# Attention loop of a two-layer MQA + SwiGLU kernel: exponentials in fixed tiles, and waits declared away

## The chip, the cores and the metric

One core of a Trainium2 chip runs the kernel. The metric is device time in microseconds of one execution of the program; less is better. TensorE is called PE (its weight loads PEld), VectorE DVE, ScalarE ACT, GpSimd POOL and SyncE SP, as in the profile. Each engine takes its own instructions in order and is held only by semaphores that other instructions raise.

## The reference

The input is x, 2048 rows of 448 floats. Two layers, with the same weights, each run attention and then a feed-forward:

```python
def _A_ref(x, wq, wk, wv, wo):          # H = 16 heads of Dh = 28; one k and one v for all heads
    q = (x @ wq).reshape(B, S, H, Dh).transpose(0, 2, 1, 3)
    k = x @ wk
    v = x @ wv
    scores = einsum("bhqd,bkd->bhqk", q, k) * (Dh ** -0.5)
    p = softmax(scores)
    o = einsum("bhqk,bkd->bhqd", p, v)
    return o.transpose(0, 2, 1, 3).reshape(B, S, H * Dh) @ wo
def _B_ref(x, w_gate, w_up, w_down):
    return (silu(x @ w_gate) * (x @ w_up)) @ w_down
for _ in range(2):
    x = x + _A_ref(layernorm(x), wq, wk, wv, wo)
    x = x + _B_ref(layernorm(x), w_gate, w_up, w_down)
```

So each layer takes 16 x 2048 x 2048 exponentials, 67 million.

## The kernel before

**Stages.** `forward` runs, for each of the two layers, projections of q, k and v (`Attention.project`), the attention loop (`Attention.scores`) and the feed-forward (`FeedForward.rest`). It is traced twice: the first version is the one that runs; a second one, with exact row maxima, stands in a branch that is taken only if the first finds a sum out of range.

**The attention loop.** Queries are taken in 16 groups `GR`: a group is a block of 512 query rows and four heads. Keys are taken in 16 tiles of 128. A *cycle* is two key tiles of one group, so a group has 8 cycles (`NT // 2`) and a layer 128. Scores are computed transposed: keys on the partitions, queries along the row. For one key tile, four heads run side by side in four row groups of PE (32 rows each, DH = 28 and the rest for the split parts); each of the four products is the sum of three matmuls, because q and k are split in a high and a low part. That makes 12 matmuls of 32 x 128 by 512 (line 590, in `tile_scores`).

**Where scores go.** PSUM has eight banks. Two tiles `threes[0]` and `threes[1]` hold three banks each: heads 0 to 2 of the first and of the second key tile of a cycle. Head 3 goes to a single bank; two single banks (6 and 7) change places from cycle to cycle (`singles`).

**The exponentials,** in `cycle(m)`, per cycle and in this order on ACT: line 607 takes the first key tile's single bank to `pt1`, line 608 its three banks to `pt` (1536 elements on each of 128 partitions), line 611 the second key tile's three banks, and line 612 the second single, in place in SBUF, after DVE has copied it there out of its bank (line 610). The copy frees the bank early. Results lie in SBUF tiles `pt` (128 x 1536) and `pt1` (128 x 512) from a pool `at{layer}` with four buffers each. A key tile takes one buffer of each, so a buffer is used again after two cycles.

**P-V.** After the scores and exponentials of cycle m have been issued, `pv(m - 1, singles(m)[0])` is issued: 8 matmuls (line 639) that multiply the exponentials of the previous cycle with `vsb`, the four heads side by side in column groups, into the single bank that line 607 of cycle m has just read. Then DVE takes the result out: at the first cycle of a group by a copy into a fresh accumulator (line 646), at the seven others by an addition (line 648). `vsb` has a column of ones, so the sum of exponentials comes along. After a group's last cycle `post` normalizes the accumulator (POOL line 677, DMA).

**What PE runs, in order:** the 12 scores of the first key tile, the 12 of the second, the 8 matmuls of the previous cycle's P-V, and so on. After certain cycles an out-projection of a finished block of rows (line 575, `outproj`) stands between two cycles; there are three in a layer's loop, and the fourth follows it.

**Who waits for whom in the loop.**
- Line 607 waits for the last scores of the first key tile; line 611 for those of the second; line 612 for the copy at line 610, which waits for the second key tile's single.
- The first scores wait until line 608 of the cycle before has read `threes[0]`, the second until line 611 has read `threes[1]`.
- P-V waits for the exponentials of the cycle before and, since it overwrites the bank, for line 607 of its own cycle.
- The second key tile's single scores of the next cycle overwrite the bank that P-V used, so they wait for the sum at line 648 or 646.

**How waits come about.** The order on each engine is that of the program text (`manual_schedule`). The framework follows which instruction reads and writes which tile and gives each instruction the waits that these need. It also does so between instructions of one engine, and does not drop a wait because another wait implies it. An instruction carries one wait; further ones stand in an event instruction (EVENT_SEMAPHORE) ahead of it. Before the change the exponentials also wait for the exponential that wrote the same buffer two cycles earlier, and the sum for the sum before it and for line 607, which read the same bank.

Of the kernel before, what the change touches and what calls it, by code (L numbers as in the profile page):

```python
# [8 lines left out]
F32 = mybir.dt.float32  # L9
F32R = mybir.dt.float32r  # L10
AF = mybir.ActivationFunctionType
ALU = mybir.AluOpType
# [3 lines left out]
P = 128  # L16
# [11 lines left out]
SCALE = DH ** -0.5  # L28
# [27 lines left out]
def forward(  # L56
# [14 lines left out]
    nc = tc.nc  # L71
# [16 lines left out]
    phase, banks, threes, live, turn = ExitStack(), [], [], set(), {}  # L88
# [33 lines left out]
    def halves(name):  # L122

        return pers.tile([P, 2, 512], F32R, tag="halves", name=name, bufs=2)
# [204 lines left out]
    class Attention:  # L329
# [224 lines left out]
        def scores(self, ff):  # L554
            next(switch)
            with tc.tile_pool(name=f"at{self.layer}", bufs=1, reuse_waits="tile") as wp:
                woh = wp.tile([P, NG, D], F32R, name="woh")
                wol = wp.tile([P, NG, D], F32R, name="wol")
                on, accs, pts = {}, {}, {}
# [23 lines left out]
                def tile_scores(n, three, one):  # L583

                    i, kt = divmod(n, NT)
                    q, k, ks = qts[i % 3], keys[kt // 4], slice(P * (kt % 4), P * (kt % 4) + P)
                    for z, (kp, part) in enumerate(((0, 0), (1, 0), (0, 1))):
                        for j in range(4):
                            js = slice(32 * j, 32 * j + 32)
                            nc.tensor.matmul(  # L590
                                three[:, j, :] if j < 3 else one, k[js, kp, ks], q[js, part, :],
                                start=(z == 0), stop=(z == 2), tile_position=(32 * j, 0),
                            )
                    pt = wp.tile([P, 3, 512], F32, name="pt", bufs=4)
                    pt1 = wp.tile([P, 512], F32, name="pt1", bufs=4)
                    pts[n] = [*(pt[:, j, :] for j in range(3)), pt1]
                    return pt, pt1

                def singles(m):

                    return banks[6 + m % 2], banks[7 - m % 2]

                def cycle(m):

                    a, b = singles(m)
                    pt, pt1 = tile_scores(2 * m, threes[0], a)
                    nc.scalar.activation(pt1, a, AF.Exp, scale=SCALE)
                    nc.scalar.activation(pt, threes[0], AF.Exp, scale=SCALE)  # L608
                    pt, pt1 = tile_scores(2 * m + 1, threes[1], b)
                    nc.vector.tensor_copy(pt1, b)  # L610
                    nc.scalar.activation(pt, threes[1], AF.Exp, scale=SCALE)  # L611
                    nc.scalar.activation(pt1, pt1, AF.Exp, scale=SCALE)

                def between_cycles(m):

# [17 lines left out]
                def pv(m, to):  # L633

                    i, u = divmod(m, NT // 2)
                    for y in range(2):
                        n = 2 * m + y
                        for j in range(4):
                            nc.tensor.matmul(  # L639
                                to[32 * j : 32 * j + 32, :], vsb[:, n % NT, :], pts[n][j],  # L640
                                start=(y == 0), stop=(y == 1), skip_group_check=True,
                            )
                        del pts[n]
                    if u == 0:
                        accs[i] = halves("o2").bitcast(F32)
                        nc.vector.tensor_copy(accs[i][:, 0, :], to)
                    else:
                        nc.vector.tensor_tensor(accs[i][:, 0, :], to, accs[i][:, 0, :], ALU.add)  # L648
                    if u == NT // 2 - 1:
                        due[m + 3] = post(i)  # L650

                def post(i):

                    c, g = GR[i]
                    out2 = accs.pop(i)
                    oraw, rb = out2[:, 0, :], out2[:, 1, :]
                    rs = wp.tile([P, 16], F32, name="rs", bufs=2)
                    for j in range(4):
                        nc.sync.dma_start(rs[32 * j : 32 * j + 32, :], oraw[32 * j + DH : 32 * j + DH + 1, :])

                    def rest():
                        if fine is not None:
                            under = wp.tile([P, 16], F32, name="under", bufs=2)
                            for bound, op in ((LIMIT, ALU.is_lt), (1.0 / LIMIT, ALU.is_gt)):
                                nc.vector.tensor_scalar(under, rs, bound, None, op)
                                nc.vector.tensor_tensor(fine, fine, under, ALU.mult)
                        nc.vector.reciprocal(rs, rs)
                        rd = dram.tile([4, 512], F32, name="rd", bufs=2)
                        nc.sync.dma_start(rd.rearrange("j (p n) -> (j p) n", n=16), rs)
                        nc.sync.dma_start(rb, rd[:, None, :].to_broadcast([4, 32, 512]))  # L670
                        if g == 0:
                            on[c] = (
                                wp.tile([P, NG, 512], F32R, name="onh"),
                                wp.tile([P, NG, 512], F32R, name="onl"),
                            )
                        oh, ol = on[c]
                        nc.gpsimd.tensor_tensor(rb, oraw, rb, ALU.mult)  # L677
                        split(oh[:, g, :], ol[:, g, :], rb)
                        if g == NG - 1 and c < NC - 1:
                            todo.append(c)  # L680

                    return rest
# [37 lines left out]
                for m in range(last):  # L720
                    i, u = divmod(m, NT // 2)
                    if u == 2 and 2 < i + 2 < len(GR):
                        self.stack(i + 2)
                    if u == 3 and 2 < i + 2 < len(GR):
                        self.parts(i + 2)
                    if u == 4 and 2 < i + 2 < len(GR) and not full:
                        self.rows(i + 2)
                    if i in (2, 3) and u == 4:
                        load_wo(i - 2)
                    if m == NT // 2 and ff.nxt:  # L730
                        ff.nxt.below(nc.sync)
                    if u == 4 and 10 < i <= 11 + FG:
                        ff.W[i - 11] = weights(i - 11)
                    cycle(m)
                    if m:
                        pv(m - 1, singles(m)[0])
                    elif not full:
                        self.maxima(NC - 1, banks[6])
                    if m in due:
                        due.pop(m)()  # L740
                    if m in aside:
                        aside[m]()
                    between_cycles(m)
                pv(last - 1, banks[6])
                self.lent = None
                next(switch)
# [258 lines left out]
    for c in range(1, NC):  # L1005
        fs, got = norm_steps(c)
        n = 4 * c - 4
# [38 lines left out]
```

## Time and profile before

| | |
|---|---|
| median of three runs | 1998.7 us |
| the three runs | 1998.66, 1998.7, 2002.25 us |
| profiled execution | 2002.23 us, of which its span 2000.5 us |
| mean granted TensorE clock | 0.997 |
| instructions recorded | 44597 |
| attention loops (first score to last P-V) | about 64 to 571 us and 1055 to 1561 us |

An *execution* is the device's own time; the *span* is from the first to the last recorded instruction of the profiled one. A record of ACT or DVE in an ordered view has a start, a duration, the engine, the source line, the operation, the tile written and the tiles read, and in brackets the idle time of the engine before it with what ended it. Start plus duration is the end. Records of one engine may overlap, as an engine begins an instruction before the one ahead has written its last result. `x8` behind a line counts merged instructions. Lines with `ACTq` or `DVEq` are instructions of an engine's queue that do no arithmetic; the page does not count them as busy.

### The profile page before, as it was taken

How to read it: one execution, taken by the hardware profiler on the slowest of the kernel's cores; microseconds unless marked ns; L12 is line 12 of the kernel's file. 1: busy time of each engine (PE TensorE's matmuls, PEld its weight loads, DVE VectorE, ACT ScalarE, POOL GpSimd, SP SyncE). 2: the span in 40 equal slices, each digit the busy share in tenths (PEclk: the TensorE clock that was granted, in tenths of full speed). 3: DMA queues.
4: the chain of work that ended last, by engine and by line, in shares of the span. 5: the costliest groups of instructions: out<-in, count | busy, mean ns of one | idle time of the engine just before them, and what ended most of it. 6: DMA issues, size and time to landing. Idle time of an engine off the chain costs nothing.

```text
span 2000.5 us, 44597 instructions
## 1 busy us (share of the span) xinstructions
PE 1978.4 (99%) x18517; PEld 1337.5 (67%) x18517; DVE 785.4 (39%) x1370; ACT 1277.5 (64%) x2142; POOL 560.4 (28%) x611
## 2 busy tenths in 40 slices
PE   9999999999999999999999999999999999999998
PEld 7544545445468999999884444454454789988887
DVE  6444443443543222322464334535444332222322
ACT  4899797997953333333349998979979433333332
POOL 5222213122214233333351221122221233233320
PEclk9999999999999999999999999999999999999999
DMA  5101020021211011110031010200212100011102
GB/s 164 52 24 37 12 57 17 22 51 32 44 42 35 25 32 31 32 31 22 12 100 35 25 31 12 62 13 26 52 37 58 45 16 22 26 31 32 32 1 76
DMA packets 126343, 75.30 MB, mean 38 GB/s; under 512 B 69656, under 2 KB 109976, under 8 KB 126136
## 3 DMA queue, kind: packets, MB, share of 16 engines
q1 hardware_dynamic: 124584, 71.20, 12.9%
q8 instruction: 146, 2.39, 0.5%
q10 hardware_dynamic: 1552, 1.20, 0.2%
q14 instruction: 61, 0.50, 0.1%
HBM read 54.01 MB, written 17.83 MB: 36 GB/s over the span
## 4 chain that ended last, share of the span: by engine, by line
PE 94%; DVE 2%; POOL 1%; ACT 1%; DMA 1%; issue 0%; ACTq 0%; POOLq 0%; SPq 0%; DVEq 0%
PE bank L318 39%; PE bank L639 24%; PE three L590 17%; PE bank L590 6%; PE bank L298 4%; PE three L575 2%; PE bank L575 2%; PE bank L248 1%; POOL xl L279 0%; DMA qd<-stage 0%; ACT pt L611 0%; DVE xn L230 0%; DMA xn<-xt 0%; DMA xres<-in_A_x_dram 0%; DVE xres L579 0%
## 5 line engine op out<-in xcount | busy, mean ns | idle before, releaser
L639 PE MATMUL bank<-pt,vsb 128*32 128x512 f32 x4096 | 493.2, 598 | 0.5
L590 PE MATMUL bank<-qstack,keys 32*128 32x512 f32 x1536 | 483.8, 424 | 1.7 <-DVE xres L579 1.7
L590 PE MATMUL three<-qstack,keys 32*128 32x512 f32 x4608 | 448.8, 420 | 1.4 <-ACT stage L524 1.0
L318 PE MATMUL bank<-xh,wgh 64*128 64x512 f32 x1728 | 443.7, 391 | 4.0 <-ACT xh L278 1.4
L590 PEld LDWEIGHTS three<-qstack,keys 32*128 32x128 f32 x4608 | 258.1, 182 | 282.2 <-ACT pt L608 185.2
L611 ACT ACTIVATE pt<-three 128x1536 f32<-128x1536 f32 x256 | 383.1, 1496 | 0.0
L608 ACT ACTIVATE pt<-three 128x1536 f32<-128x1536 f32 x256 | 379.4, 1482 | 0.0
L318 PE MATMUL bank<-xh,wgl 64*128 64x512 f32 x1404 | 366.2, 391 | 0.0
L318 PE MATMUL bank<-wdh,h 64*128 64x448 f32 x1792 | 333.1, 365 | 1.2 <-ACT h L904 0.8
L318 PE MATMUL bank<-xl,wgh 64*128 64x512 f32 x1296 | 331.4, 391 | 2.6 <-POOL xl L279 2.1
L903 DVE TENSOR_TENSOR sg<-bank,sg 128x512 f32<-128x512 f32 x112 | 77.5, 692 | 511.8 <-ACT sg L902 502.6
L318 PEld LDWEIGHTS bank<-xh,wgh 64*128 64x128 f32 x1728 | 261.2, 185 | 22.5 <-POOL xh L288 2.2
L639 PEld LDWEIGHTS bank<-pt,vsb 128*32 128x32 f32 x4096 | 107.1, 109 | 249.1 <-issue 152.6
L810 POOL TENSOR_TENSOR xres<-stage,xres 128x448 f32<-128x448 f32 x108 | 127.9, 1204 | 506.0 <-ACT stage L809 506.0
L648 DVE TENSOR_TENSOR o<-bank,o 128x512 f32<-128x512 f32 x224 | 155.0, 692 | 280.5 <-PE bank L639 276.4
L610 DVE COPY pt<-bank 128x512 f32<-128x512 f32 x256 | 176.9, 691 | 205.5 <-PE bank L590 203.1
L318 PEld LDWEIGHTS bank<-wdh,h 64*128 64x128 f32 x1792 | 244.3, 185 | 14.7 <-issue 2.3
L590 PEld LDWEIGHTS bank<-qstack,keys 32*128 32x128 f32 x1536 | 243.9, 183 | 7.8 <-DVE xres L579 3.6
L677 POOL TENSOR_TENSOR o<-o 128x512 f32<-128x512 f32 x32 | 41.2, 1289 | 739.7 <-DMA o<-rd 431.6
L325 ACT COPY seen<-bank 128x1 f32<-128x1 f32 x664 | 81.4, 163 | 255.0 <-PE bank L318 249.8
L318 PEld LDWEIGHTS bank<-xh,wgl 64*128 64x128 f32 x1404 | 214.7, 185 | 13.1
L318 PE MATMUL bank<-wdl,h 64*128 64x448 f32 x896 | 218.2, 368 | 0.0
(130 smaller groups left out, 2323.5 us busy)
## 6 DMA issues: line engine op xcount, KB each, us to landing
o<-rd SPq DMA_DIRECT2D x32, 256.0 KB
qd<-stage SPq DMA_DIRECT2D x32, 224.0 KB
qraw<-qd SPq DMA_DIRECT2D x128, 56.0 KB
wdr<-in_B_w_down_dram SPq DMA_DIRECT2D x28, 224.0 KB
xt<-tb SPq DMA_DIRECT2D x96, 56.0 KB
wr<-in_B_w_gate_dram SPq DMA_DIRECT2D x28, 192.0 KB
wr<-in_B_w_up_dram SPq DMA_DIRECT2D x28, 192.0 KB
xn<-xt SPq DMA_DIRECT2D x6, 768.0 KB
```

Source lines behind the costliest of these rows:

```text
L298: nc.tensor.matmul(po, a, b, start=(i == 0), stop=(i == len(seq) - 1))
L318: nc.tensor.matmul(po, a, b, start=start, stop=stop, skip_group_check=True)
L325: nc.scalar.copy(seen[:, i : i + 1], po[:, 0:1])
L575: nc.tensor.matmul(po[:, 0:D], a[:, g, ts_], b[:, g, :], start=(g + z == 0), stop=(g == NG - 1 and z == 2))
L590: nc.tensor.matmul(three[:, j, :] if j < 3 else one, k[js, kp, ks], q[js, part, :], start=(z == 0), stop=(z == 2), tile_position=(32 * j, 0),)
L608: nc.scalar.activation(pt, threes[0], AF.Exp, scale=SCALE)
L610: nc.vector.tensor_copy(pt1, b)
L611: nc.scalar.activation(pt, threes[1], AF.Exp, scale=SCALE)
L639: nc.tensor.matmul(to[32 * j : 32 * j + 32, :], vsb[:, n % NT, :], pts[n][j], start=(y == 0), stop=(y == 1), skip_group_check=True,)
L648: nc.vector.tensor_tensor(accs[i][:, 0, :], to, accs[i][:, 0, :], ALU.add)
L810: nc.gpsimd.tensor_tensor(r, s, r, ALU.add)
L903: nc.vector.tensor_tensor(sg, pg[1], sg, ALU.mult)
```

## The change

Three things are changed, all in `Attention.scores`.

1. The exponentials' tiles are allocated once, before the loop, as four pairs `pt0` to `pt3` and `single0` to `single3`; key tile n of the loop uses pair n % 4. Before, each key tile asked the pool for the next of four rotating buffers.
2. Dependencies are declared away: of each exponential on the one two cycles earlier in the same buffer; of the copy at line 610 on line 612 two cycles earlier; of each sum (line 648) on the sum of the cycle before; and of each sum or first copy (648, 646) on line 607 of the cycle in which it runs.
3. Lists keep the instructions that these declarations name.

```diff
-                    pt = wp.tile([P, 3, 512], F32, name="pt", bufs=4)
-                    pt1 = wp.tile([P, 512], F32, name="pt1", bufs=4)
+                    pt, pt1 = bufs[n % 4]
                     pts[n] = [*(pt[:, j, :] for j in range(3)), pt1]
                     return pt, pt1
 
+                exps, sums = {}, {}
+                bufs = [
+                    (wp.tile([P, 3, 512], F32, name=f"pt{y}"), wp.tile([P, 512], F32, name=f"single{y}"))
+                    for y in range(4)
+                ]
+
...
                     a, b = singles(m)
                     pt, pt1 = tile_scores(2 * m, threes[0], a)
-                    nc.scalar.activation(pt1, a, AF.Exp, scale=SCALE)
-                    nc.scalar.activation(pt, threes[0], AF.Exp, scale=SCALE)
+                    es = [nc.scalar.activation(pt1, a, AF.Exp, scale=SCALE)]
+                    es.append(nc.scalar.activation(pt, threes[0], AF.Exp, scale=SCALE))
                     pt, pt1 = tile_scores(2 * m + 1, threes[1], b)
-                    nc.vector.tensor_copy(pt1, b)
-                    nc.scalar.activation(pt, threes[1], AF.Exp, scale=SCALE)
-                    nc.scalar.activation(pt1, pt1, AF.Exp, scale=SCALE)
+                    copy = nc.vector.tensor_copy(pt1, b)
+                    es.append(nc.scalar.activation(pt, threes[1], AF.Exp, scale=SCALE))
+                    es.append(nc.scalar.activation(pt1, pt1, AF.Exp, scale=SCALE))
+                    exps[m] = [e.ins for e in es]
+                    for new, old in zip(exps[m], exps.get(m - 2, ())):
+                        tc.declare_no_dep(new, old, reason="P-V, which read the buffer, waited for the old one")
+                    if m > 1:
+                        tc.declare_no_dep(copy.ins, exps[m - 2][3], reason="P-V, which read it, waited for that")
...
                     if u == 0:
                         accs[i] = halves("o2").bitcast(F32)
-                        nc.vector.tensor_copy(accs[i][:, 0, :], to)
+                        f = nc.vector.tensor_copy(accs[i][:, 0, :], to)
                     else:
-                        nc.vector.tensor_tensor(accs[i][:, 0, :], to, accs[i][:, 0, :], ALU.add)
+                        f = nc.vector.tensor_tensor(accs[i][:, 0, :], to, accs[i][:, 0, :], ALU.add)
+                        if m + 1 in exps:
+                            tc.declare_no_dep(f.ins, sums[m - 1], reason="scores, ahead of this P-V, waited for the sum")
+                    sums[m] = f.ins
+                    if m + 1 in exps:
+                        tc.declare_no_dep(f.ins, exps[m + 1][0], reason="P-V waited for the bank's exponential")
```

## The prediction

> **What bounds the kernel now.** I read the page first, for the share of each engine and for the slices, then the stretches of the attention loop, then its instructions in order of time.
>
> ```profile
> span 2000.5 us, 44597 instructions
> ...
> PE 1978.4 (99%) x18517; PEld 1337.5 (67%) x18517; DVE 785.4 (39%) x1370; ACT 1277.5 (64%) x2142; POOL 560.4 (28%) x611
> ...
> ACT  4899797997953333333349998979979433333332
> ```
>
> The change touches only the two attention stages, where ACT stands at 7 to 9 tenths (it drops where out-projections stand between cycles); over the whole span it has 64%, a mean over two kinds of stage. PE's 99% says little: its matmul ends are modelled and the records overlap. The next view is busy time in the eight stretches of uninterrupted attention cycles, four per layer, cut at the first exponential of a cycle (first stretch and sum; columns are length, then busy us and count of PE, PEld, DVE, ACT, POOL).
>
> ```profile
> 65.02:201.41 136.39, 136.01 (x1475) 58.97 (x1479) 55.66 (x98) 136.39 (x149) 26.23 (x25) 1.00 0.10 29
> ...
> sum 914.93, PE 913.74 PEld 395.01 DVE 411.87 ACT 914.60 POOL 182.42; mean PE 114.22 PEld 49.38 DVE 51.48 ACT 114.33 POOL 22.80
> ```
>
> ACT is busy 914.60 of 914.93 us. A layer has 128 cycles; three hold an out-projection and the last has no successor, so the stretches hold 2 x 124 = 248 cycles: 914.93 / 248 = 3.689 us each. Is that ACT's own rate, or another engine's pace with ACT's records stretched over it? The cycles just after an out-projection tell, where PE is well ahead (ACT in order of time: start, duration):
>
> ```profile
> 477.17 0.61 ACT L607 ACTIVATE pt<-bank 128x512 f32<-128x512 f32 x1
> 477.64 1.47 ACT L608 ACTIVATE pt<-three 128x1536 f32<-128x1536 f32 x1
> 478.97 1.49 ACT L611 ACTIVATE pt<-three 128x1536 f32<-128x1536 f32 x1
> 480.30 0.67 ACT L612 ACTIVATE pt<-pt 128x512 f32<-128x512 f32 x1
> 480.82 0.64 ACT L607 ACTIVATE pt<-bank 128x512 f32<-128x512 f32 x1
> ...
> 484.48 0.67 ACT L607 ACTIVATE pt<-bank 128x512 f32<-128x512 f32 x1
> ...
> 488.14 0.69 ACT L607 ACTIVATE pt<-bank 128x512 f32<-128x512 f32 x1
> ```
>
> By starts, L607 comes every (488.14 - 477.17) / 3 = 3.657 us. But its record grows, 0.61, 0.64, 0.67, 0.69. By ends (477.78, 481.46, 485.15, 488.83) the distance is 11.05 / 3 = **3.683 us**. Starts run ahead of what gets finished, so the ends are the rate. At finer digits the same ends repeat at 3.685 in most cycles; I use 3.685. So 248 cycles at ACT's own rate take 913.9 us, and they took 914.93: all other waits together cost about **1.05 us** of the loop.
>
> The other engines stand close behind, which the chain of waits on the page, 94% PE, hides. One cycle (all engines, in order of time):
>
> ```profile
> 301.52 1.92 PE L639 MATMUL bank<-pt,vsb 128*32 128x512 f32 x16
> ...
> 303.38 0.50 PE L590 MATMUL three<-qstack,keys 32*128 32x512 f32 x3
> ...
> 303.57 0.69 DVE L648 TENSOR_TENSOR o<-bank,o 128x512 f32<-128x512 f32 x1 [1.25 <-PE bank L639]
> ...
> 303.96 0.39 PE L590 MATMUL bank<-qstack,keys 32*128 32x512 f32 x1
> 304.12 0.19 PEld L590 LDWEIGHTS three<-qstack,keys 32*128 32x128 f32 x3 [0.21 <-ACT pt L611]
> ...
> 304.31 0.18 PEld L590 LDWEIGHTS bank<-qstack,keys 32*128 32x128 f32 x1
> ...
> 304.47 0.60 ACT L607 ACTIVATE pt<-bank 128x512 f32<-128x512 f32 x1
> ...
> 304.88 0.39 PE L590 MATMUL bank<-qstack,keys 32*128 32x512 f32 x1
> 304.96 1.45 ACT L608 ACTIVATE pt<-three 128x1536 f32<-128x1536 f32 x1
> 305.20 0.16 PEld L639 LDWEIGHTS bank<-pt,vsb 128*32 128x32 f32 x8 [0.36 <-ACT pt L607]
> ...
> 305.31 0.69 DVE L610 COPY pt<-bank 128x512 f32<-128x512 f32 x1 [1.05 <-PE bank L590]
> ```
>
> **Loop A, through the sum:** P-V starts at 301.52 and ends at 303.44; the sum L648 starts 0.13 later, ends at 304.26, and 0.05 later (304.31) the single's weights for the second scores load, since those scores overwrite the bank that the sum reads; the last score starts at 304.88 and the next P-V at 305.20. That is 3.68 us, as long as ACT's rate. **Loop B, through L607:** P-V 301.52, scores 303.38, the first twelve end at 304.35, L607 starts 0.12 later, takes 0.60 to 0.69, and P-V may follow 0.05 after its end: 1.86 + 0.97 + 0.12 + 0.60 + 0.05 = 3.60, with the long record 3.69. So three loops are within 0.1 us of each other, and ACT's is the one that cannot shrink.
>
> **The change part by part.** What can go is seen in the instructions of each line (event instructions that carry a wait of their own, counts, ns min/median/max, first and last start):
>
> ```profile
> L607 ACTq EVENT_SEMAPHORE  x254: 17/17/1029, 64.2 to 1556.6; - x127
> ...
> L611 ACTq EVENT_SEMAPHORE  x252: 17/17/17, 73.1 to 1557.3; - x126
> ...
> L612 ACTq EVENT_SEMAPHORE  x252: 17/17/17, 73.9 to 1558.2; - x126
> ...
> L648 DVEq EVENT_SEMAPHORE  x224: 21/1881/2069, 73.2 to 1560.2; - x112
> ...
> L646 DVEq EVENT_SEMAPHORE  x32: 21/50/50, 71.4 to 1537.2; - x32
> ```
>
> An instruction with more than one wait is preceded by such an event. With the wait for the exponential two cycles back gone, each of L607, L611, L612 has one wait left (PE, PE, the copy): about 758 ACT events go. L648 keeps PE alone: 224 go. L646, the first sum of eight, loses one wait but its tile must still come free.
>
> *Price of an event on the path.* L648 behind its event starts 0.13 after the last P-V; L610, which has none, starts at 305.31, 0.04 after the matmul that ends at 305.27. So 0.09 us per sum. For ACT the row without an event is the cast below: matmul end 64.03, start 64.06, 0.03 against L607's 0.12, again 0.09 (0.06 to 0.09, rounding included).
>
> ```profile
> 63.64 0.39 PE L298 MATMUL bank<-xh,wl 128*128 128x512 f32 x1
> ...
> 64.06 0.59 ACT L523 CAST q<-bank 112x512 fp32r<-112x512 f32 x1 [2.32 <-PE bank L298]
> ```
>
> Summed blindly, 224 x 0.09 = 20 us on DVE and 254 x 0.09 = 23 us on ACT. But loop A falls to 3.59 and loop B to 3.51-3.60, and ACT's 3.685 then covers both. What is left to win there is the 1.05 us.
>
> *Does ACT's rate itself fall?* The 758 events are 17 ns each, 13 us if they took engine time. They do not: the first two cycles of each layer have none for L611 and L612 (first one at 73.1), and yet:
>
> ```profile
> 65.02 0.61 ACT L607 ACTIVATE pt<-bank 128x512 f32<-128x512 f32 x1
> ...
> 68.69 0.63 ACT L607 ACTIVATE pt<-bank 128x512 f32<-128x512 f32 x1
> ...
> 72.35 0.66 ACT L607 ACTIVATE pt<-bank 128x512 f32<-128x512 f32 x1
> ```
>
> Ends 65.63, 69.32, 73.01: 3.69 per cycle, the same rate without them. I take 0 here; the bounds are 0 and, by starts, 8.0 us (rival 1).
>
> The Trainium skill (Perfetto Trace Analysis, section "DVE / Act Engine Instruction") says why in a rule that speaks against this change: a semaphore wait is served in a queue ahead of the engine, and the record runs from the first element to the acknowledged write. By that rule a wait long satisfied costs a saturated engine nothing; the stretched records with even ends agree.
>
> *The rest.* The copies' dropped wait: L610 already has a single wait's delay, and L612, which needs it, starts 1.6 us after it ends (302.32 to 303.93): 0. Restarts after the six out-projections and the two layer starts: there L607 waits on PE in the open, 8 x 0.06 = 0.5 us at most, 0.3 taken. First sums of eight (L646): if their event stays, 0.13 against the others' 0.04, 32 x 0.09 = 2.9 us without cover, 0 under ACT's slack of 0.09 per cycle. Fixed tiles: same bytes, same four buffers; ACT's ends are equally spaced whichever buffer is written: 0. Feed-forward and projections: untouched.
>
> **Sum:** about 0.7 of the 1.05 us (one or two long cycles will remain) plus 0.3 = **-1.0 us**. The profiled execution is 2002.23 us, span 2000.5 and 1.7 around it: span 1999.5, execution 2001.2. It lies 3.5 above the median of the runs, 1998.7, so for a median **1997.7 us**, -0.05%. Its own range is 1996.5 to 1999.
>
> **Rivals.**
> 1. *Starts are the rate.* If ACT can hold the 3.657 us of starts once no event stands between exponentials, 914.93 - 248 x 3.657 = 8.0 us go: 1998.7 - 8.0 - 0.3 = **1990.4**. For it: loops A and B would allow it (3.59, 3.60). Against: the growing records, and the first cycles without events.
> 2. *Nothing is taken away*, because another dependency still makes the instruction take two waits: events stay, **1998.7**. It cannot be excluded from the trace; it differs little from the forecast.
> 3. *The stage boundary, slower.* The tiles now live from before the loop to its end, in another layout, and the feed-forward's tiles lie over them. If a tile on its path comes to lie over a buffer read by the last P-V where an earlier one was read a cycle before, it waits one cycle longer, 3.7 us in each layer: 1998.7 + 7.4 = **2006.1**. It decides once the added delay exceeds 2 us per layer. Against it: what the feed-forward's first copies wait for is the out-projection, which PE runs after the last P-V.
>
> ```profile
> ACT xh L278 <- PE bank L575: 8.5, 2, 4.5
> ```
>
> **How the numbers follow.** Forecast 0.58, rival 1 0.25, rival 2 0.05, rival 3 0.12. About 0.2%, 4 us, is what a measurement of this kernel can tell from no change. Faster: rival 1, 0.25. Same: forecast and rival 2, 0.63. Slower: rival 3, 0.12. The range takes in the forecast, rivals 1 and 2: 1990.3 to 2001, the upper end with 2 us for a boundary that costs a little.
>
> **What would show it.** Right: events of L611, L612 and L648 gone; the sum 0.04 after P-V; L607's record near its longest (0.70) in most cycles, since ACT alone now paces; L607's ends still 3.685 apart; 248 cycles in 914 us. Wrong: ends under 3.67 (rival 1); event counts unchanged (rival 2); a later first feed-forward matmul relative to the last P-V (rival 3); or P-V waiting for something other than L607.

## The result and the profile after

The changed kernel takes 1999.16 us (median of 12 runs, 1997.58 to 2001.18); the kernel before, run beside it, 2000.99 us (12 runs, 1998.66 to 2003.03). The ratio is 0.9992, with a 95% interval from 0.9983 to 1.0: no change that can be told with confidence, with a lean of 0.1% towards faster. The profiled execution of after took 1999.73 us, its span 1998.0; that of before 2002.23 and 2000.5. Some 2.5 us have to be found in the traces.

In after the lines have moved: the four exponentials are 612 (was 607), 613, 616 and 617 (was 612), the copy is 615, the sum 658 (was 648), the first sum of a group 656, P-V 649 (was 639). Scores stay at 590.

**What was taken away.** The lines of after, with their instructions (count, ns min/median/max, first and last start):

```profile
L612 ACT ACTIVATE single<-bank x256: 597/754/762, 65.3 to 1554.7; 128x512 f32<-128x512 f32 x128
L612 ACTq EVENT_SEMAPHORE  x8: 17/17/17, 64.5 to 1461.5; - x8
...
L616 ACT ACTIVATE pt<-three x256: 1461/1614/1633, 67.2 to 1556.5; 128x1536 f32<-128x1536 f32 x128
...
L617 ACT ACTIVATE single<-single x256: 642/799/808, 68.5 to 1557.8; 128x512 f32<-128x512 f32 x128
...
L658 DVEq EVENT_SEMAPHORE  x2: 21/21/21, 568.6 to 1558.2; - x2
...
L656 DVEq EVENT_SEMAPHORE  x28: 21/21/21, 130.7 to 1535.4; - x28
```

The first single's exponential had 254 events and has 8; lines 616 and 617 had 252 each and have no row for events at all; the sum had 224 and has 2. So 750 events went from ACT and 222 from DVE, and the declarations do what they say. The first exponential's own record was shorter in before:

```profile
L607 ACT ACTIVATE pt<-bank x256: 597/627/700, 65.0 to 1556.6; 128x512 f32<-128x512 f32 x128
```

**The rate of the loop.** Two rows of the first exponential, from the ordered view of ACT, 37 uninterrupted cycles apart, in after:

```profile
65.34 0.61 ACT L612 ACTIVATE single<-bank 128x512 f32<-128x512 f32 x1
...
201.56 0.76 ACT L612 ACTIVATE single<-bank 128x512 f32<-128x512 f32 x1
```

and in before, where the first of the two rows is the one at 65.02 in the prediction:

```profile
201.41 0.60 ACT L607 ACTIVATE pt<-bank 128x512 f32<-128x512 f32 x1
```

Ends are what counts, since the record of after has grown from 0.61 to 0.76 us on the way: 202.32 - 65.95 = 136.37 us in after, 202.01 - 65.63 = 136.38 us in before. Both are 3.686 us per cycle. Without a single event between its exponentials ACT holds the rate that it had with three per cycle. From end to end (medians over the loops) its four exponentials take 487, 1340, 1344 and 514 ns in after, together 3.685 us, and 488, 1341, 1344 and 512 in before. Over all 248 uninterrupted cycles the ends are 914.26 us apart in after and 914.97 in before.

**One cycle in the middle of after** (start, duration, engine, line; in brackets the idle time and what ended it):

```profile
300.73 0.76 ACT L612 ACTIVATE single<-bank 128x512 f32<-128x512 f32 x1
301.22 1.60 ACT L613 ACTIVATE pt<-three 128x1536 f32<-128x1536 f32 x1
301.54 0.12 PEld L649 LDWEIGHTS bank<-pt,vsb 128*32 128x32 f32 x3 [0.42 <-ACT single L612]
...
302.55 1.62 ACT L616 ACTIVATE pt<-three 128x1536 f32<-128x1536 f32 x1
...
302.87 0.59 PE L649 MATMUL bank<-single,vsb 128*32 128x512 f32 x1
...
303.53 0.69 DVE L658 TENSOR_TENSOR o<-bank,o 128x512 f32<-128x512 f32 x1 [1.25 <-PE bank L649]
...
303.88 0.81 ACT L617 ACTIVATE single<-single 128x512 f32<-128x512 f32 x1
...
304.42 0.75 ACT L612 ACTIVATE single<-bank 128x512 f32<-128x512 f32 x1
```

No ACT row has a bracket: the engine is never idle. P-V's weights load 0.05 us after line 612 ends (301.49), so P-V waits for ACT and for nothing else; the sum follows the last P-V (303.46) by 0.07 where it took 0.13. PE now waits for ACT, and DVE for PE. Line 612's record grows because its start follows the scores, while its end keeps ACT's distance: the one at 304.42 starts 0.27 us before the exponential ahead of it, line 617, ends at 304.69.

**Where the difference sits.** What ACT waited for, at the six places where an out-projection stands between two cycles (us in total, times, longest), in before:

```profile
ACT pt L607 <- PE bank L590: 64.2, 6, 10.8
```

and in after:

```profile
ACT single L612 <- PE bank L590: 62.8, 6, 10.6
```

1.4 us less. Cut by the first exponentials' ends and starts, the span differs by 0.71 in the 248 uninterrupted cycles, by 1.40 at the six out-projections, and by 0.7 in the tail behind the last loop (440.06 to 439.38), less 0.3 at the start (first exponential at 65.02, now 65.34). The stretch from the last exponential of the first layer to the first of the second is the same: 485.81 and 485.79. Of the tail's 0.7, 0.5 is the spread of the kernel before itself: a second profile of it has 439.56.

The six out-projections fall into two parts. Their 48 matmuls take 9.81 or 9.63 us from the first start to the last in these two kernels; before has 9.81 five times of six, after twice. Which pace a given place gets changes from one execution to the next of the same kernel: a second profile of before has 9.81 three times, of after never. So 3 x 0.187 = 0.56 of the 1.40 lies in the pace. Whether that is all chance is not shown: over two profiles of each kernel, 9.81 stands at 8 of 12 places in before and at 2 of 12 in after. The rest repeats and is the change's: outside these matmuls an episode, from the end of the last first exponential to the end of the next, takes 4.72 us on average in both profiles of before and 4.58 in both of after, 0.14 less, and 6 x 0.14 = 0.84.

### The profile page after: what moved, and what is told of

Same layout as the page of the kernel before. It is cut to its first block, busy times and chain, and to the rows that moved or that the text cites. A ratio compares the mean times of both kernels' runs of the same rounds, so it can differ in the third digit from the quotient of the medians.

```text
span 1998.0 us, 43621 instructions
## 1 busy us (share of the span) xinstructions
PE 1974.9 (99%) x18517; PEld 1311.8 (66%) x18517; DVE 783.7 (39%) x1370; ACT 1277.2 (64%) x2142; POOL 560.5 (28%) x611
## 4 chain that ended last, share of the span: by engine, by line
PE 95%; DMA 1%; DVE 1%; POOL 1%; ACT 1%; issue 0%; ACTq 0%; POOLq 0%; SPq 0%; DVEq 0%
PE bank L318 38%; PE bank L649 24%; PE three L590 20%; PE bank L298 5%; PE bank L590 3%; PE three L575 2%; PE bank L575 2%; PE bank L248 1%; DMA xn<-xt 1%; POOL xl L279 0%; DMA qd<-stage 0%; DMA wr<-in_B_w_up_dram 0%; PE bank L424 0%; DMA xres<-in_A_x_dram 0%; DVE xres L579 0%
## 5 line engine op out<-in xcount | busy, mean ns | idle before, releaser
L649 PE MATMUL bank<-single,vsb 128*32 128x512 f32 x1024 | 487.4, 598 | 0.0
L590 PE MATMUL bank<-qstack,keys 32*128 32x512 f32 x1536 | 470.8, 424 | 1.7 <-DVE xres L579 1.7
L590 PE MATMUL three<-qstack,keys 32*128 32x512 f32 x4608 | 461.9, 425 | 1.3 <-ACT stage L524 0.9
L590 PEld LDWEIGHTS three<-qstack,keys 32*128 32x128 f32 x4608 | 251.9, 183 | 294.8 <-ACT pt L613 184.3
L616 ACT ACTIVATE pt<-three 128x1536 f32<-128x1536 f32 x256 | 409.1, 1598 | 0.0
L613 ACT ACTIVATE pt<-three 128x1536 f32<-128x1536 f32 x256 | 405.5, 1584 | 0.0
L649 PEld LDWEIGHTS bank<-pt,vsb 128*32 128x32 f32 x3072 | 101.7, 109 | 260.3 <-issue 152.5
L615 DVE COPY single<-bank 128x512 f32<-128x512 f32 x256 | 176.9, 691 | 207.8 <-PE bank L590 205.5
L612 ACT ACTIVATE single<-bank 128x512 f32<-128x512 f32 x256 | 187.9, 734 | 62.9 <-PE bank L590 62.8
```

The lines of the kernel that those rows point to most:

```text
L590: nc.tensor.matmul(three[:, j, :] if j < 3 else one, k[js, kp, ks], q[js, part, :], start=(z == 0), stop=(z == 2), tile_position=(32 * j, 0),)
L612: es = [nc.scalar.activation(pt1, a, AF.Exp, scale=SCALE)]
L613: es.append(nc.scalar.activation(pt, threes[0], AF.Exp, scale=SCALE))
L615: copy = nc.vector.tensor_copy(pt1, b)
L616: es.append(nc.scalar.activation(pt, threes[1], AF.Exp, scale=SCALE))
L649: nc.tensor.matmul(to[32 * j : 32 * j + 32, :], vsb[:, n % NT, :], pts[n][j], start=(y == 0), stop=(y == 1), skip_group_check=True,)
```

## The experiments

In the diffs, lines are those of the changed kernel unless it is said otherwise. Of all loops the time is given by ends of the first exponential over the same 248 cycles.

### Both kernels once more

The changed kernel in eleven more runs, and the kernel before in one more profiled execution.

> The changed kernel once more, to see what of its trace repeats. Theory (ACT's own rate bounds the loop; the waits taken away lay under it): L612's ends 3.685 to 3.687 us apart, the 248 uninterrupted cycles in 914.0 to 914.6 us, P-V's weights 0.05 us after the end of L612, each out-projection 0.09 to 0.14 us shorter measured from the last exponential's end to the next one's, and now and then 0.19 us more; span 1.5 to 3 us below that of the kernel before. Rival (a part of the gain is one execution's chance): the out-projections and the P-V gap scatter as much as before, and the span is within 1 us of 2000.5.

> The kernel before once more, to see how far its out-projections and its few long cycles are one execution's chance. Theory (the 0.14 us per out-projection that lies outside its matmuls is the change's; the pace of the matmuls themselves, 9.63 or 9.81 us, is not): outside the matmuls 4.71 to 4.73 us again, matmuls of both paces, the 248 cycles 914.3 to 915.3 us. Rival (both belong to the kernel): five of six out-projections at the long pace again, and 4.7 us outside.

The changed kernel: 1999.93 against 2002.23 us, ratio 0.9988, interval 0.9979 to 0.9997. This time the interval lies below 1. Its span was 1997.5; that of the kernel before, 2000.8. The loops repeat: 914.25 (first profile 914.26) and 914.98 (914.97), and so do the episodes without their matmuls, 4.58 and 4.72. These two figures therefore separate the kernels far better than the times, which spread over 3.5 to 7.3 us within one set of runs of one kernel.

### One half at a time

The sums' and the copies' declarations without the exponentials':

```diff
-                    for new, old in zip(exps[m], exps.get(m - 2, ())):
-                        tc.declare_no_dep(new, old, reason="P-V, which read the buffer, waited for the old one")
```

> Fixed tiles, the sums' and the copies' waits declared away, the exponentials' waits on older exponentials kept: events stand ahead of L612 and L616. Theory: the sum starts 0.04 to 0.07 us after P-V, so the loop through the sum falls under ACT's rate; the loop through L612 is 1.86 + 0.97 + 0.12 + 0.69 + 0.05 = 3.69 us, level with ACT; ends 3.685 to 3.689 apart; P-V 0.05 us after the end of L612; out-projections 0.09 us shorter than before, since P-V comes earlier, and L612 still starts 0.09 after the scores there. Time -0.5 to -1.5 us. Rival (the events on ACT's queue are what costs): as the kernel before, within 0.3 us, and the whole gain in the other half.

The exponentials' without the sums' and the copies':

```diff
-                    if m > 1:
-                        tc.declare_no_dep(copy.ins, exps[m - 2][3], reason="P-V, which read it, waited for that")
...
-                        if m + 1 in exps:
-                            tc.declare_no_dep(f.ins, sums[m - 1], reason="scores, ahead of this P-V, waited for the sum")
...
-                    if m + 1 in exps:
-                        tc.declare_no_dep(f.ins, exps[m + 1][0], reason="P-V waited for the bank's exponential")
```

> Fixed tiles and the exponentials' waits declared away, the sums' waits kept: no events on ACT, an event ahead of each sum. Theory: the loop through the sum stays 3.68 us with its 0.13, level with ACT's rate; ends 3.686 to 3.690 apart; P-V 0.10 to 0.17 us after the end of L612 as before; out-projections 0.05 us shorter (L612 starts 0.04 and not 0.09 after the scores). Time 0 to -0.7 us. Rival (events on ACT's queue are what costs): ends below 3.680 apart and -2 us or more.

Times: the sums' half 2000.94 us, ratio 0.9994 (0.9985 to 1.0003); the exponentials' half 2001.45, ratio 0.9998 (0.9989 to 1.0007). Neither differs from the kernel before by what can be measured, and the two cannot be told apart by time: the one profile of the exponentials' half has the shortest span of all full kernels, 1996.7, of which 1.2 us is a shorter stretch between the layers that no other run has. The traces do tell them apart. The sums' half, by line:

```profile
L612 ACT ACTIVATE single<-bank x256: 597/693/707, 65.0 to 1555.1; 128x512 f32<-128x512 f32 x128
L612 ACTq EVENT_SEMAPHORE  x254: 17/17/1029, 64.1 to 1555.0; - x127
```

and the exponentials' half, whose sum is line 656:

```profile
L612 ACT ACTIVATE single<-bank x256: 597/652/762, 64.8 to 1553.6; 128x512 f32<-128x512 f32 x128
L612 ACTq EVENT_SEMAPHORE  x8: 17/17/17, 63.9 to 1460.4; - x8
...
L656 DVEq EVENT_SEMAPHORE  x224: 21/1881/1908, 72.9 to 1557.2; - x112
```

How the six out-projections go, worked out from the instructions of each trace (us, medians of six; P-V's first load after the last first exponential's end, then from the first scores behind the out-projection to the start of the first exponential, then the whole episode, end to end, without the out-projection's own matmuls):

| kernel | P-V after the exponential | scores to exponential | rest of an episode | 248 cycles |
|---|---|---|---|---|
| before | 0.14 | 1.83 | 4.73 | 914.97 |
| sums' half | 0.05 | 1.84 | 4.63 | 914.72 |
| exponentials' half | 0.21 | 1.78 | 4.74 | 914.25 |
| after | 0.05 | 1.78 | 4.58 | 914.26 |

The 0.14 us of an episode is thus made of two: 0.09 because P-V no longer lags behind the loop's last exponential (the sums' half alone has it), and 0.05 because the first exponential follows its scores sooner (the exponentials' half alone has it: 0.05 after them where it was 0.12). The sums' half does not have the second. The exponentials' half has it, but there P-V falls further behind, 0.21: the exponential ends sooner, and PE, still held by the sums' waits, does not come sooner. The gain is lost again: its episodes were expected 0.05 shorter and are no shorter than before's. Of the loop's 0.7 us the exponentials' half alone has all, the sums' half 0.25.

### Fixed tiles alone

This was meant to be the changed kernel with the sums' two declarations alone, and the expectation speaks of that. What ran declares nothing at all: it holds the fixed tiles only. The kernel that the expectation describes was run afterwards, and comes next.

```diff
-                    for new, old in zip(exps[m], exps.get(m - 2, ())):
-                        tc.declare_no_dep(new, old, reason="P-V, which read the buffer, waited for the old one")
-                    if m > 1:
-                        tc.declare_no_dep(copy.ins, exps[m - 2][3], reason="P-V, which read it, waited for that")
...
-                        if m + 1 in exps:
-                            tc.declare_no_dep(f.ins, sums[m - 1], reason="scores, ahead of this P-V, waited for the sum")
...
-                    if m + 1 in exps:
-                        tc.declare_no_dep(f.ins, exps[m + 1][0], reason="P-V waited for the bank's exponential")
```

> Fixed tiles, the sums' and the exponentials' waits: copies and exponentials declared nothing, the sums' two declarations kept. The order on each engine is unchanged. Theory: as sums_only, since the copies' declaration hides nothing that is late: the copy may wait for the exponential two cycles back, 3 us old by then. Its event makes the copy start 0.12 and not 0.04 us after the scores, and its result is needed 1.6 us later: time within 0.5 us of sums_only. Rival (the copy's wait matters, because DVE no longer learns of ACT from the sums): ends 3.69 or more apart and 1 us or more slower than sums_only.

2001.58 us, ratio 0.9995 (0.9986 to 1.0004); 248 cycles in 915.27. Its lines:

```profile
L612 ACT ACTIVATE single<-bank x256: 597/648/706, 64.9 to 1557.1; 128x512 f32<-128x512 f32 x128
L612 ACTq EVENT_SEMAPHORE  x254: 17/17/1027, 64.1 to 1557.1; - x127
...
L617 ACT ACTIVATE single<-single x256: 641/696/750, 68.1 to 1560.3; 128x512 f32<-128x512 f32 x128
...
L654 DVEq EVENT_SEMAPHORE  x224: 21/1881/1909, 73.1 to 1560.7; - x112
```

Line 617 has no row for events here either: fixed tiles alone take the 252 events of the in-place exponential away, and nothing in the time follows that can be told. All others stay, and the copy still has none. In the trace two small things cancel: the loop is 0.30 us longer than in before, and the episodes of the out-projections take 4.68 us, 0.04 less each, 0.25 in six. P-V follows the exponential there by 0.07 to 0.14 us, so a part of the 0.09 above may belong to the fixed tiles; this is one profile. As a whole the fixed tiles neither cost nor win what can be measured, and what the change wins beyond them comes from the declarations.

### The copies' declaration

The sums' declarations on the fixed tiles, without those of exponentials and copies:

```diff
-                    for new, old in zip(exps[m], exps.get(m - 2, ())):
-                        tc.declare_no_dep(new, old, reason="P-V, which read the buffer, waited for the old one")
-                    if m > 1:
-                        tc.declare_no_dep(copy.ins, exps[m - 2][3], reason="P-V, which read it, waited for that")
```

> Fixed tiles; the sums' two declarations kept; those of the copies and the exponentials left out. Theory: the copy now waits for the exponential two cycles back, 3 us old by then, behind an event: it starts 0.09 to 0.12 and not 0.04 us after the scores, and its result is needed 1.6 us later; everything else as in sums_only: cycles 3.685 to 3.690 us by ends, P-V 0.05 us after L612's end, 248 cycles 914.2 to 915.0 us. Rival (DVE, no longer told of ACT by the sums, holds the bank too long): cycles 3.70 or more.

One profiled execution: 2001.0 us, beside 2002.25 for the kernel before; 248 cycles in 915.04.

```profile
L615 DVE COPY single<-bank x256: 652/692/693, 66.1 to 1556.7; 128x512 f32<-128x512 f32 x128
L615 DVEq EVENT_SEMAPHORE  x246: 21/21/21, 73.0 to 1556.6; - x123
```

The copy gets an event here that it had neither in the rotating pool nor on fixed tiles with all waits kept: it appears once the sums' waits are declared away and the copy's is not. With it the copy starts 0.107 us after its scores instead of 0.037 (medians). The cycle hardly moves: 915.04 against 914.72 with the declaration is 0.001 us per cycle, and one execution does not tell whether that is the copy's. Line 617 starts 1.6 us after the copy ends (the two ends in the prediction), and that hides 0.07.

### ACT made lighter, in both kernels

The claim that tells most is that the waits have a price, and that ACT's own rate hides it. So ACT was given less to do: the fourth exponential is left out, and the copy writes max(score, 0) + 1 in its place. In the kernel before (lines of before):

```diff
-                    nc.vector.tensor_copy(pt1, b)
+                    nc.vector.tensor_scalar(pt1, b, 0.0, 1.0, ALU.max, ALU.add)
...
-                    nc.scalar.activation(pt1, pt1, AF.Exp, scale=SCALE)
```

> The kernel before with a quarter of ACT's instructions taken away: the fourth exponential of a cycle (L612) is left out, and the DVE copy ahead of it writes max(score, 0) + 1 in its place, so that the sums stay positive. ACT's rate by ends falls from 3.685 to 0.487 + 1.340 + 1.344 = 3.17 us. Theory (ACT is the bound by a hair, the loop through the sum is right under it): the cycle falls by next to nothing, to 3.68 to 3.70 us, because the sum's loop (1.92 + 0.13 + 0.69 + 0.05 + 0.57 + 0.32 = 3.68) takes over; time within 3 us of the kernel before. Rival (the loop through the sum has slack, and ACT alone paces): 3.2 to 3.5 us per cycle, 45 us or more faster.

In the changed kernel the same, and the copy's declaration names the copy two cycles back, which is now the writer of that buffer:

```diff
-                exps, sums = {}, {}
+                exps, sums, copies = {}, {}, {}
...
-                    copy = nc.vector.tensor_copy(pt1, b)
+                    copy = nc.vector.tensor_scalar(pt1, b, 0.0, 1.0, ALU.max, ALU.add)
...
-                    es.append(nc.scalar.activation(pt1, pt1, AF.Exp, scale=SCALE))
...
+                    copies[m] = copy.ins
...
-                        tc.declare_no_dep(copy.ins, exps[m - 2][3], reason="P-V, which read it, waited for that")
+                        tc.declare_no_dep(copy.ins, copies[m - 2], reason="P-V, which read it, waited for that")
```

> The changed kernel with the same fourth exponential left out and the same DVE operation in its place; the copies' declaration names the copy two cycles back. Theory: without ACT above them, the waits taken away show their full price: the sum starts 0.04 to 0.07 after P-V, its loop is 3.59 to 3.62 us and paces; 248 cycles x 0.06 to 0.09 = 15 to 22 us faster than before_light, where the full kernels differ by 2. Rival (the waits cost nothing anywhere, because other waits end later): the same as before_light within 3 us.

The light kernel before takes 2000.22 us, ratio to the full kernel before 0.9992 (0.9982 to 1.0001). The light changed kernel takes 1987.11 us, ratio 0.993 (0.9909 to 0.995). The 37 cycles of the first stretch, in the light kernel before:

```profile
68.50 0.61 ACT L607 ACTIVATE pt<-bank 128x512 f32<-128x512 f32 x1
...
205.17 0.60 ACT L607 ACTIVATE pt<-bank 128x512 f32<-128x512 f32 x1 [0.42 <-PE bank L590]
```

and in the light changed kernel:

```profile
64.90 0.61 ACT L612 ACTIVATE single<-bank 128x512 f32<-128x512 f32 x1
...
199.20 0.60 ACT L612 ACTIVATE single<-bank 128x512 f32<-128x512 f32 x1 [0.36 <-PE bank L590]
```

136.66 us by ends, 3.694 per cycle, and 134.29, 3.629. ACT is no longer the bound in either. The later row of each has idle time ahead of it, the record is back at 0.60, and the view of busy time over the same stretch of the light changed kernel (length, then busy time of PE, PEld, DVE, ACT and POOL with instructions) shows ACT busy for 121 of 134 us:

```profile
64.90:199.20 134.30, 133.94 (x1472) 59.16 (x1476) 55.65 (x98) 121.44 (x113) 26.42 (x25) 1.00 0.11 30
```

The kernel before loses 0.51 us of ACT's work in each cycle and does not get faster: over 248 cycles 914.96 us, where the full one has 914.97. What paces it then is the loop through P-V and the sum, at 3.689, within 0.004 of ACT's 3.685. Only when the waits are gone as well does the cycle fall, to 3.6345: 901.37. The difference between the two light kernels, 13.59 us or 0.055 per cycle, is the price of the removed waits when ACT's rate no longer covers it, somewhat less than the 15 to 22 that were expected. In size it is the sum's 0.124 - 0.068 = 0.056 us (medians). With ACT's full work, the same removal yields 0.7.

That it is the sum's wait, and not those of the exponentials, shows in the parts of the loop (medians, us, over the cycles with a sum): from the start of P-V to its end, then to the sum's start, the sum itself, from its end to the weights of the single's scores, and on to the next P-V.

| kernel | P-V | to the sum | sum | to the weights | to the next P-V | P-V after the exponential |
|---|---|---|---|---|---|---|
| light before | 1.925 | 0.124 | 0.691 | 0.052 | 0.887 | 0.147 |
| light changed | 1.925 | 0.068 | 0.692 | 0.053 | 0.893 | 0.152 |
| after | 1.925 | 0.069 | 0.692 | 0.052 | 0.948 | 0.050 |

Only the step to the sum differs between the light kernels. In both, P-V starts 0.15 us after the first exponential's end, where a P-V that waits for ACT starts 0.05 after it (last row): the exponentials are not on the path. Behind a group's first copy, whose event stays, a cycle of the light changed kernel still takes 3.69 us against 3.63 otherwise.

The page of waits agrees. DVE's waits at the sum (us in total, times, longest), light kernel before:

```profile
DVE o L647 <- PE bank L638: 278.5, 222, 1.6
```

Light changed kernel:

```profile
DVE o L658 <- PE bank L649: 265.2, 223, 1.2
```

13.3 us less of waiting for P-V, about as much as the cycles fell.

### Moving work from ACT to POOL

If ACT is the bound, the next step is to give part of its exponentials to another engine. POOL is 28% busy and can raise a number to a power:

```diff
-                    es.append(nc.scalar.activation(pt1, pt1, AF.Exp, scale=SCALE))
+                    es.append(nc.scalar.activation(pt1[:, 0:448], pt1[:, 0:448], AF.Exp, scale=SCALE))
+                    nc.gpsimd.tensor_tensor(pt1[:, 448:512], grow.to_broadcast([P, 64]), pt1[:, 448:512], ALU.pow)
```

`grow` holds the number e to the power of the scale.

> The changed kernel with 64 of the 512 columns of the fourth exponential taken from ACT and computed on POOL, as a constant to the power of the score, in place behind the copy. ACT's rate falls by 64 x 0.00083 = 0.053 us to 3.632 us, where the loop through the sum stood in after_light. Theory: if POOL's power takes under 2.5 us for 64 columns, cycles of 3.63 to 3.65 us, 9 to 13 us less. Rival: POOL's power costs what its 4 columns do at line 223 (1.0 us, 0.8 more than the plain operation on 4 columns at line 222), 0.2 us per column, so 13 us; P-V waits for it, and the cycle is 13 us or more, 3 ms for the kernel.

3977.34 us, beside 2002.25 for the kernel before. From the page's list of costliest groups (busy, mean ns of one, then idle time and what ended it):

```profile
L620 POOL TENSOR_TENSOR single<-grow,single 128x64 f32<-128x64 f32 x256 | 2686.4, 10522 | 34.8 <-DVE single L617 34.6
```

Each takes 10.5 us, nearly three cycles, for an eighth of one exponential that ACT does in 0.51, and a cycle now lasts 10.65 us by ends: the expectation's rival held, at a price somewhat below its 13 us. At 0.164 us per column, if the time goes by columns, POOL could carry 22 columns within a cycle of 3.69 us, with nothing else to do. ACT needs 0.833 ns per column (its steps from end to end are 487 ns for 512 columns and 1340 for 1536), so this would save 18 ns of a cycle at most. No version faster than both kernels was found.

## Why the prediction came out as it did

**ACT's rate is the bound, by ends.** Shown. The prediction took 3.685 us per cycle from ends against 3.657 from starts, and expected the ends to stay and line 607's record to grow. Ends are 3.686 with and without events; the record grew from 627 to 754 ns, more than the 0.70 forecast. The Trainium skill (Perfetto Trace Analysis, section "DVE / Act Engine Instruction") has an instruction's semaphore wait in a queue ahead of the engine, from which the prediction drew that a wait already satisfied costs a saturated engine nothing. The trace agrees: 750 events of 17 ns are 12.8 us, and the loop lost 0.7.

**The loops behind ACT.** Shown, with one size off. The prediction had P-V through the sum at 3.68 and ACT at 3.685, and said that ACT would cover what the former loses. The light kernels show both: taking work from ACT wins nothing while the waits are there, and taking the waits away wins 0.7 us while ACT has its full work. The price of the sum's wait was taken as 0.09, by likening the sum to the copy, which starts 0.04 after its matmul. Without its event the sum starts 0.07 after, so the price is 0.055: 13.6 us over 248 cycles with ACT made lighter, not 20. On ACT the event's price was taken as 0.09, or 0.06 at the restarts, and is 0.06.

**The 0.7 us of the loop.** Forecast 0.7, measured 0.71. That the size is met is partly luck. Of 0.71, some 0.32 is long cycles, 0.2 to 0.3 us longer than the rest: before has two among its 248 in both of its profiles, at the 124th and the 177th cycle, after has one, at the 235th, in both of its. The remaining 0.4 is spread thinly over the other cycles. The exponentials' half has no long cycle and yet the same sum as after, so long cycles alone do not decide it. Why a given place of the program has a long cycle was not settled: the queue that the profile names `instruction` moved 61 packets in before and 54 in after, but 56 in the exponentials' half.

**The restarts.** This term was too small: 0.3 forecast, 0.84 measured (6 x 0.14). Its own part was right, 0.05 per out-projection for a first exponential that follows its scores sooner, 6 x 0.05 = 0.3. What the step overlooked is that PE reaches the out-projection sooner as well. In the loop PE ran as late as the sum let it, and P-V stood 0.14 behind the exponential when the loop broke off; now it stands 0.05 behind. Slack won inside the loop is worth next to nothing there, but at each break it is paid out once, 6 x 0.09 = 0.54. A further 0.56 of the profiled difference is the pace of the out-projections' matmuls, for which the prediction had no term; whether the change has a part in it stays open.

**Copies, tiles, first sums: 0.** Shown for the tiles, and for the copies too, with a detail that the prediction had not seen: once the sums' waits are declared away, the copy gets a second wait, and starts 0.07 us late, so its declaration keeps a delay away rather than removing one. The first sums kept 28 of their 32 events, at no cost in the full kernel's cycle.

**The rivals.** Starts as the rate would have given ends near 3.657 without events: they are 3.686, so it is out. Nothing taken away: 254, 252, 252 and 224 events became 8, 0, 0 and 2. A slower stage boundary: the stretch between the layers is 485.8 in both (487.2 and 485.9 in the second profiles), the tail behind the second loop is not longer, and what the feed-forward's first pieces wait for in after is still the out-projection, as before:

```profile
ACT xh L278 <- PE bank L575: 8.8, 2, 4.4
```

**The sum.** Forecast -1.0 us; by the traces 0.71 + 0.84 = 1.55 us of the 2.5 between the two profiled executions repeat and are the change's, the rest being the pace of the out-projections and the spread of the tail and the start. The paired medians differ by 1.8 in one set of runs and 2.3 in the other, each with an interval some 3.5 us wide. The forecast median of 1997.7 was missed, and its own range of 1996.5 to 1999 by 0.2: after has 1999.16. It started from 1998.7, the median of three runs of before, and twelve give 2000.99. So the level was off by the base, and the difference came out larger than forecast, by the restarts above all.

## What to carry to other kernels

When two loops are within a few thousandths of each other, neither an engine's work nor the waits of the other loop can be priced by taking one away: take both away once, and the difference shows the hidden price (here 13.6 us, of which 0.7 can be had). Read the rate of a saturated engine from the ends of its records, since starts drift ahead as records grow (3.657 against 3.686 us per cycle here). Slack won behind the bound was paid out here only where the loop breaks off (0.09 us at each of six breaks), so count the breaks.

## What was not expected of the hardware

- An event for a second wait costs more than its record. Records are 17 and 21 ns, yet with it the instruction behind starts 0.06 us later on ACT (0.116 against 0.052 after the scores) and 0.055 to 0.07 later on DVE (sum 0.124 against 0.068; copy 0.107 against 0.037). On ACT, which is behind, its ends stay 3.686 us apart with and without events.
- Even with one wait, the sum starts 0.07 after the matmul that it waits for, the copy 0.04. The runs do not show why.
- The 48 matmuls of an out-projection mostly take 9.63 or 9.81 us (four of 60 places lie between), changing from execution to execution of the same kernel, at a granted clock that the rows show as full (1.00). The longer pace stands at 11 of 18 places in the kernels with rotating buffers and at 7 of 42 in those with fixed tiles. The runs do not show why.
- A power on POOL takes 10.5 us for 128 x 64, which is 0.164 us per column.
